# Square, cast and subtraction over two blocks at a time, the second layer in runs of a pair, and row-tiled matmuls behind the last block

## The chip, the cores and the metric

The kernel runs on one core of a Trainium2 chip. TensorE multiplies; VectorE, ScalarE and GpSimd work on tiles in SBUF, the on-chip memory; TensorE writes its results to PSUM, a second on-chip memory of eight banks; SyncE issues the transfers. Each engine takes its instructions in the order in which the program lists them, and waits at an instruction until what it needs is there. The metric is the device time of one execution, in microseconds (us); the profile describes one execution of the program.

## The reference

Four batches of 12480 tokens with 128 channels pass through an attention with 49 agents per batch, and the result goes through a layer with squared relu (d_ff = 2048).

```python
def _attn_ref(q, k, v, agents):
    scale = 1.0 / np.sqrt(q.shape[-1])
    def sm(a, b):
        s = scale * (a @ b.transpose(0, 2, 1))
        s = s - s.max(-1, keepdims=True)
        e = np.exp(s)
        return e / (e.sum(-1, keepdims=True) + 1e-09)
    agent_v = sm(agents, k) @ v
    return sm(q, agents) @ agent_v

def _moe_ref(x, w_in, w_out):
    r = np.maximum(x @ w_in, 0.0)
    return (r * r) @ w_out
```

## The kernel before

**Tiling.** The tokens are cut into 52 stages (NSG) of 960 tokens, 13 per batch, and the 2048 hidden columns into 16 blocks (NF) of 128. The main loop counts blocks: i = 16 * stage + block, 832 in all. A tile of a block holds 128 hidden columns by 960 tokens, as two halves of 480, one PSUM bank each. The values are split in two: a number rounded to the fast matmul type (the high half) and the remainder (the low half), and a product is made of three matmuls: high by high, high by low, low by high.

**One pair of blocks.** `mm1` (line 340) makes the hidden values of blocks i and i+1 in one go: four full matmuls and four that use 32 rows of the array each, side by side. `relu` (354) takes a block out of PSUM on ScalarE, `square` (358) squares it on ScalarE, `high` (362) makes the rounded copy `gh` on VectorE and `low` (366) the remainder `gl` on VectorE. `mm2` (370) multiplies `gh` and `gl` of one block with the second layer's weights `wo_hi` and `wo_lo` and adds into two PSUM banks `out0` and `out1`, six matmuls per block. The first and last block of a stage do the three products of one half and then those of the other; the blocks between do four with `wo_hi` and then two with `wo_lo`. After the last block `store` (392) copies the two banks out, one on ScalarE and one on VectorE, and sends them off. There is one pair of `out` banks, so the next stage's first `mm2` waits for these copies.

**The order.** Nothing is scheduled by a tool: every step is entered with a time by `at` (408), the list is sorted by that time (597), and each engine gets its instructions in this order. Times are in units of blocks, so a period of the loop is two units, from an even i to the next. Lines 583 to 595 enter the steps of the main loop; `mm2` and `store` follow the block by LAG = 4 units.

**The attention.** It is laid between the steps of the main loop. A planner (`chain`, 418; `plan_tokens`, 452; `plan_batch`, 461) gives each step a slot g, a whole number, and enters it at g + .5; no engine has two such steps in a slot. For each stage, `plan_tokens` enters in the slots of the stage before: scores on TensorE (`q_scores`) and `q_max` on VectorE in slot 16n, `q_sub` on VectorE in 16n+1, `q_exp` on ScalarE and `q_sum` on VectorE in 16n+2, `q_inverse` on VectorE in 16n+4, then GpSimd and ScalarE steps, `q_transpose` on TensorE and two `q_copy` on ScalarE in 16n+10 and 16n+11. `plan_batch` spreads the next batch's work over a whole batch: `k_scores`, `k_copy`, `k_pmax` first, then `v_hi` and `v_lo` (ScalarE, VectorE), `v_acc` (TensorE), `v_sum` (VectorE), at the end `a_final` and the folded weights `w_make`. In the last batch only token work is left.

**Buffers.** The pool `ew` holds the tiles of the main loop by tag: `r` (2 buffers), `g` (3), `gh` and `gl` (4 each), of 960 columns. At the start the same buffers serve the weights, which arrive as 64-bit numbers: `raw_load` (71) fetches a piece, `to_f32` (80) turns it into 32 bit on VectorE with work tiles `cv_p` and `cv_x`.

Of the kernel before, what the change touches and what calls it, by code (L numbers as in the profile page):

```python
# [9 lines left out]
F32 = mybir.dt.float32  # L10
BF16 = mybir.dt.bfloat16
F32R = mybir.dt.float32r
U32 = mybir.dt.uint32
AF = mybir.ActivationFunctionType
ALU = mybir.AluOpType
AX = mybir.AxisListType

P = 128
CH = 120
G = 8  # L20
TT = CH * G // 2
# [4 lines left out]
def agent_attention_relu2_kernel(ctx: ExitStack, tc: tile.TileContext, qT, kT, v, agT, w_in, w_out, outT):  # L26
# [6 lines left out]
    nc = tc.nc  # L33
    C, B, NCH, _ = kT.shape
    A = agT.shape[2]
    F = w_in.shape[1]
    NF = F // P
    NS = NCH // G
    A2 = 2 * A
    scale = 1.0 / math.sqrt(C)  # L40

    cpool = ctx.enter_context(tc.tile_pool(name="cpool", bufs=1))
    io = ctx.enter_context(tc.tile_pool(name="io", bufs=6))
    wk = ctx.enter_context(tc.tile_pool(name="wk", bufs=2))
    ew = ctx.enter_context(tc.tile_pool(name="ew", bufs=4))
    ps_h = ctx.enter_context(tc.tile_pool(name="ps_h", bufs=2, space=bass.MemoryType.PSUM))
    ps_o = ctx.enter_context(tc.tile_pool(name="ps_o", bufs=1, space=bass.MemoryType.PSUM))
    ps_a = ctx.enter_context(tc.tile_pool(name="ps_a", bufs=2, space=bass.MemoryType.PSUM))
# [13 lines left out]
    win_sb = cpool.tile([P, F], F32, name="win_sb")  # L62
    wo_hi = cpool.tile([P, NF, P], F32R, name="wo_hi")
    wo_lo = cpool.tile([P, NF, P], F32R, name="wo_lo")
    PW = 512
# [3 lines left out]
    raws = {}  # L69

    def raw_load(t, src):
        raw = ew.tile([P, PW, 2], U32, name="raw", tag="gl")
        raws[t, src is wi_bits] = raw
        if src is wi_bits:
            nc.sync.dma_start(out=raw, in_=wi_bits[:, t * PW:(t + 1) * PW, :])
        else:
            nj = PW // P
            nc.sync.dma_start(out=raw.rearrange("p (j c) w -> p j c w", c=P), in_=wo_bits[:, t * nj:(t + 1) * nj])

    def to_f32(raw, dst):  # L80

        lo, hi = raw[:, :, 0], raw[:, :, 1]
        p = ew.tile([P, PW], U32, name="cv_p", tag="g", bufs=3)
        x = ew.tile([P, PW], F32, name="cv_x", tag="gh")
        ts, stt = nc.vector.tensor_scalar, nc.vector.scalar_tensor_tensor
        return [
            lambda: ts(out=p, in0=hi, scalar1=20, scalar2=0x7FF, op0=ALU.logical_shift_right, op1=ALU.bitwise_and),
            lambda: ts(out=p, in0=p, scalar1=896.0, scalar2=1151.0, op0=ALU.max, op1=ALU.min),  # L90
            lambda: ts(out=p, in0=p, scalar1=896.0, scalar2=float(1 << 23), op0=ALU.subtract, op1=ALU.mult),
            lambda: stt(out=p, in0=hi, scalar=0x80000000, in1=p, op0=ALU.bitwise_and, op1=ALU.bitwise_or),
            lambda: ts(out=x.bitcast(U32), in0=hi, scalar1=0xFFFFF, scalar2=0x100000, op0=ALU.bitwise_and, op1=ALU.bitwise_or),
            lambda: stt(out=x, in0=lo, scalar=2.0 ** -32, in1=x.bitcast(U32), op0=ALU.mult, op1=ALU.add),
            lambda: stt(out=dst, in0=x, scalar=2.0 ** -20, in1=p.bitcast(F32), op0=ALU.mult, op1=ALU.mult),
        ]

    cv, wo = {}, {}

    def win_make(t, step):  # L100
        if step == 0:
            cv["i"] = to_f32(raws.pop((t, True)), win_sb[:, t * PW:(t + 1) * PW])
        cv["i"][step]()

    def wo_make(t, step):
        if step == 0:
            wo[t] = ew.tile([P, PW], F32, name="wo_f", tag="gh")
            cv["o"] = to_f32(raws.pop((t, False)), wo[t])
        cv["o"][step]()

    def wo_split(t, step):
# [20 lines left out]
    kts, vts, pes, pss = {}, {}, {}, {}  # L132
# [4 lines left out]
    def bank():  # L137
        turn[0] += 1
        if many[0] and turn[0] % 2:
            return ps_h.tile([P, 2, 512], F32, name="h")[:, 0]  # L140
        return ps_a.tile([P, 512], F32, name="ps_att")
# [106 lines left out]
    X = 28  # L248
    R = A - X
    K = A2 + X  # L250
    assert K <= P and R <= 32
    W = {}
    w_lo = cpool.tile([A, F], F32R, name="w_lo")

    def w_make(b, f, step):
        sl = slice(f * 512, (f + 1) * 512)
        if f == 0 and step == 0:
            W[b] = (wk.tile([P, F], F32R, name="w_a"), wk.tile([P, NF // 2, P], F32R, name="w_b"))
        wa, wb = W[b]
        if step == 0:  # L260
            pss["w", f] = bank()
            nc.tensor.matmul(pss["w", f][:A2, :], a2, win_sb[:, sl], start=True, stop=True)  # L262
        elif step == 1:
            nc.scalar.copy(wa[:A2, sl], pss["w", f][:A2, :])
        elif step == 2:
            nc.vector.tensor_tensor(w_lo[:, sl], pss.pop(("w", f))[:A, :], wa[:A, sl].bitcast(F32), op=ALU.subtract)
        else:
            nc.sync.dma_start(out=wa[A2:K, sl].bitcast(F32), in_=w_lo[:X, sl].bitcast(F32))
            for r in range(4):
                src = w_lo[X:, sl].rearrange("a (j u p) -> a j u p", u=2, p=P)[:, :, r // 2]  # L270
                eng = nc.scalar if b == 0 and f == 0 and r > 1 else nc.sync
                eng.dma_start(out=wb[32 * r:32 * r + R, 2 * f:2 * f + 2].bitcast(F32), in_=src.bitcast(F32))


    PT, qs, es, mxs, sms, pps = {}, {}, {}, {}, {}, {}
# [57 lines left out]

    NSG = B * NS
    NG = NSG * NF
    hs, rs_, gs, ghs, gls = {}, {}, {}, {}, {}

    outs = {}

# [11 lines left out]
            nc.tensor.matmul(hs[i + r // 2][:, r % 2, :TT], wb[rows, i % NF // 2, :], pb[rows], start=False, stop=True)  # L351

    def relu(i):
        rs_[i] = ew.tile([P, 2, TT], F32, name="r", bufs=2)
        nc.scalar.activation(rs_[i], hs.pop(i)[:, :, :TT], AF.Relu)  # L355

    def square(i):
        gs[i] = ew.tile([P, 2, TT], F32, name="g", bufs=3)
        nc.scalar.activation(gs[i], rs_.pop(i), AF.Square)  # L359

    def high(i):
        ghs[i] = ew.tile([P, 2, TT], F32R, name="gh")
        nc.vector.tensor_copy(ghs[i], gs[i])  # L363

    def low(i):
        gls[i] = ew.tile([P, 2, TT], F32R, name="gl")
        nc.vector.tensor_tensor(out=gls[i], in0=gs.pop(i), in1=ghs[i].bitcast(F32), op=ALU.subtract)  # L367

    def mm2(i):
        s, j = divmod(i, NF)  # L370
        gh, gl = ghs.pop(i), gls.pop(i)
        if j == 0:
            outs[s] = [ps_o.tile([P, 512], F32, name=f"out{t}") for t in range(2)]
        o = outs[s]
        first, last = j == 0, j == NF - 1

        def one(w, x, t, st=False, sp=False):
            nc.tensor.matmul(o[t][:, :TT], w[:, j, :], x[:, t, :], start=st, stop=sp)  # L378

        if first or last:  # L380
            for t in range(2):
                one(wo_hi, gh, t, st=first)
                one(wo_lo, gh, t)
                one(wo_hi, gl, t, sp=last)
        else:
            for t in range(2):
                one(wo_hi, gh, t)
                one(wo_hi, gl, t)
            for t in range(2):
                one(wo_lo, gh, t)  # L390

    def store(s):
        o = outs.pop(s)
# [10 lines left out]
    LAG = 4  # L404
# [3 lines left out]
    def at(t, f, *args):  # L408
        steps.append((t, len(steps), f, args))
# [8 lines left out]
    def chain(t, todo):  # L418
# [29 lines left out]
        return first, t  # L448

    reads_bank = (k_copy, k_pmax, k_max, v_sum, a_final, w_make, q_max, q_sub, q_copy)  # L450

    def plan_tokens(s, base, loaded=False):
# [55 lines left out]
    for n, x, src in ((0, .025, wi_bits), (1, .055, wi_bits), (2, .085, wi_bits), (3, .125, wi_bits),  # L508
                      (0, .325, wo_bits), (1, .355, wo_bits), (2, .385, wo_bits), (3, .415, wo_bits)):
        at(Z + x, raw_load, n, src)  # L510
    for n in range(NS):
        t = Z + 6 + KP * n
# [4 lines left out]
    for x in range(7):  # L517
        for n in range(3):
            at(Z + (9 if (n, x) != (2, 6) else 18) + 6 * n + .8 * x, win_make, n, x)
# [14 lines left out]
    for n in range(NS):  # L534
        t = t0 + 1.84 * n
# [3 lines left out]
    for x in range(7):  # L539
        at(t0 + 2 + .7 * x, win_make, 3, x)  # L540
        for n in range(3):
            at(t0 + 7 + 5 * n + .7 * x, wo_make, n, x)
# [24 lines left out]
    for x in range(7):  # L567
        at(t + 5.5 + .1 * x, wo_make, 3, x)
# [6 lines left out]
    for f in range(2, F // 512):  # L575
        _, e = chain(4 * f - 7, [("PE", w_make, 0, f, 0), ("ACT", w_make, 0, f, 1), ("DVE", w_make, 0, f, 2)])
# [3 lines left out]
    for b in range(1, B):  # L580
        plan_batch(b, (b - 1) * NS * NF, NS * NF)

    for i in range(NG + LAG):
        if i < NG:
            if i % 2 == 0:
                at(i, mm1, i)
                at(i + .1, relu, i)
                at(i + .12, relu, i + 1)
            at(i + .55, square, i)
            at(i + .6, high, i)  # L590
            at(i + (.65 if i % 2 else 1.25), low, i)
        if 0 <= i - LAG < NG:
            at(i + .2, mm2, i - LAG)
            if (i - LAG) % NF == NF - 1:
                at(i + .2, store, (i - LAG) // NF)
    with tc.manual_schedule():
        for _, _, f, args in sorted(steps, key=lambda x: x[:2]):
            f(*args)
# [24 lines left out]
```

## Time and profile before

| | |
|---|---|
| median of 3 runs | 2048.43 us (2046.95 to 2049.32) |
| span of the profiled execution | 2044.0 us |
| granted TensorE clock, mean over the span | 0.997 |
| data moved | 125.16 MB, 61 GB/s on the mean |

The span runs from the first to the last instruction of the profiled execution. "Busy" is the time in which an engine works on an instruction; matmuls overlap one another in the record, so TensorE's busy time alone does not say how near its peak it is. A row of the list of groups gives the source line, engine and operation, what it writes and reads, its shape and its count, then busy time and the mean duration of one instruction in ns, then the engine's idle time ahead of it and who ended it. A row of the timeline gives start, duration, engine, line and operation; "x4" stands for four instructions in a row, and a bracket for idle time ahead of it and what ended that. A row of the busy time by stretch gives the stretch, its length, the busy time (and count) of TensorE, its weight loads, VectorE, ScalarE and GpSimd, then the granted TensorE clock, the share of the DMA engines and GB/s.

### The profile page before, as it was taken

How to read it: one execution, taken by the hardware profiler on the slowest of the kernel's cores; microseconds unless marked ns; L12 is line 12 of the kernel's file. 1: busy time of each engine (PE TensorE's matmuls, PEld its weight loads, DVE VectorE, ACT ScalarE, POOL GpSimd, SP SyncE). 2: the span in 40 equal slices, each digit the busy share in tenths (PEclk: the TensorE clock that was granted, in tenths of full speed). 3: DMA queues.
4: the chain of work that ended last, by engine and by line, in shares of the span. 5: the costliest groups of instructions: out<-in, count | busy, mean ns of one | idle time of the engine just before them, and what ended most of it. 6: DMA issues, size and time to landing. Idle time of an engine off the chain costs nothing.

```text
span 2044.0 us, 30401 instructions
## 1 busy us (share of the span) xinstructions
PE 2024.0 (99%) x11011; PEld 1581.1 (77%) x11017; DVE 1823.7 (89%) x2274; ACT 1729.4 (85%) x2166; POOL 230.2 (11%) x196
## 2 busy tenths in 40 slices
PE   9899999999999999999999999999999999999999
PEld 8678777777777777777778787777777777777777
DVE  7688899999888889999998888999998988989897
ACT  2587889998887888999888888999888888888897
POOL 0100002221000001222100000122210000000000
PEclk9899999999999999999999999999999999999999
DMA  9321212211121212211112211212101111111010
GB/s 312 91 79 54 74 51 63 84 51 35 56 70 53 83 46 68 74 57 58 35 50 76 76 52 60 72 57 70 56 26 50 45 31 45 30 34 39 28 35 25
DMA packets 51446, 125.16 MB, mean 61 GB/s; under 512 B 7072, under 2 KB 16560, under 8 KB 51296
## 3 DMA queue, kind: packets, MB, share of 16 engines
q1 hardware_dynamic: 51198, 123.19, 19.5%
q8 instruction: 86, 1.41, 0.3%
q14 instruction: 64, 0.52, 0.1%
q10 hardware_dynamic: 98, 0.04, 0.0%
HBM read 81.37 MB, written 25.56 MB: 52 GB/s over the span
## 4 chain that ended last, share of the span: by engine, by line
PE 86%; DVE 8%; issue 4%; DMA 1%; ACT 1%; SPq 0%; DVEq 0%; ACTq 0%
PE out L378 51%; PE h L348 16%; PE h L351 8%; PE ps_att L154 3%; PE ps_att L285 3%; DVE gh L363 3%; DVE gl L367 2%; PE ps_att L322 1%; PE ps_att L209 1%; DVE vs L202 1%; DMA vt<-v 1%; PE ps_att L262 1%; PE h L154 0%; ACT g L359 0%; DVE ob L396 0%
## 5 line engine op out<-in xcount | busy, mean ns | idle before, releaser
L367 DVE TENSOR_TENSOR gl<-g,gh 128x960 fp32r<-128x960 f32 x832 | 1016.5, 1222 | 30.6
L355 ACT ACTIVATE r<-h 128x960 f32<-128x960 f32 x832 | 763.8, 974 | 175.9 <-PE h L351 172.2
L359 ACT ACTIVATE g<-r 128x960 f32<-128x960 f32 x832 | 825.3, 1016 | 5.2 <-DVE gl L367 5.2
L378 PE MATMUL out<-gh,wo_hi 128*128 128x480 f32 x1664 | 689.9, 415 | 5.1 <-DVE ob L396 3.6
L363 DVE CAST gh<-g 128x960 fp32r<-128x960 f32 x832 | 583.3, 701 | 97.1 <-ACT g L359 84.5
L378 PE MATMUL out<-gl,wo_hi 128*128 128x480 f32 x1664 | 633.7, 381 | 1.4 <-DVE gl L367 1.0
L378 PE MATMUL out<-gh,wo_lo 128*128 128x480 f32 x1664 | 516.1, 381 | 0.0
L348 PE MATMUL h<-p_a,w_a 126*128 126x480 f32 x1664 | 435.2, 383 | 1.8 <-ACT r L355 1.8
L378 PEld LDWEIGHTS out<-gh,wo_hi 128*128 128x128 f32 x1664 | 313.2, 188 | 141.3 <-issue 71.0
L378 PEld LDWEIGHTS out<-gh,wo_lo 128*128 128x128 f32 x1664 | 312.9, 188 | 49.3
L348 PEld LDWEIGHTS h<-p_a,w_a 126*128 126x128 f32 x1664 | 309.1, 189 | 52.8 <-ACT r L355 2.7
L378 PEld LDWEIGHTS out<-gl,wo_hi 128*128 128x128 f32 x1664 | 313.8, 189 | 41.6 <-DVE gl L367 5.7
L351 PE MATMUL h<-p_b,w_b 21*128 21x480 f32 x1664 | 204.9, 479 | 0.7 <-DMA w_b<-w_lo 0.7
L308 POOL TENSOR_TENSOR e<-e,sm 120x392 f32<-120x392 f32 x52 | 55.0, 1059 | 1322.0 <-DVE sm L305 1197.3
L351 PEld LDWEIGHTS h<-p_b,w_b 21*128 21x128 f32 x1664 | 80.1, 181 | 139.6 <-issue 137.9
L285 PEld LDWEIGHTS ps_att<-ag_sb,qt 128*120 128x120 f32 x832 | 95.2, 185 | 3.7 <-issue 0.2
L285 PE MATMUL ps_att<-ag_sb,qt 128*120 128x49 f32 x832 | 92.7, 264 | 0.0
L154 PEld LDWEIGHTS ps_att<-ag_sb,kt 128*120 128x120 f32 x704 | 80.6, 185 | 3.2 <-PE ps_att L262 0.3
L190 POOL TENSOR_TENSOR pe<-sk,pe 120x392 fp32r<-120x392 f32 x39 | 52.7, 1351 | 235.2 <-ACT pe L187 193.3
L154 PE MATMUL ps_att<-ag_sb,kt 128*120 128x49 f32 x704 | 78.4, 264 | 0.1
L158 ACT COPY sk<-ps_att 120x392 f32<-120x392 f32 x44 | 21.4, 487 | 63.7 <-PE ps_att L154 63.7
L315 POOL TENSOR_TENSOR pp<-e,pp 120x392 fp32r<-120x392 f32 x52 | 55.6, 1070 | 163.2 <-ACT pp L312 158.9
(93 smaller groups left out, 939.5 us busy)
## 6 DMA issues: line engine op xcount, KB each, us to landing
vt<-v SPq DMA_DIRECT2D x104, 243.8 KB
kt<-kT SPq DMA_DIRECT2D x52, 480.0 KB
qt<-qT SPq DMA_DIRECT2D x52, 480.0 KB
outT<-ob SPq DMA_DIRECT2D x51, 480.0 KB
p_b<-p_a SPq DMA_DIRECT2D x208, 39.4 KB
p_a<-p_a SPq DMA_DIRECT2D x52, 105.0 KB
raw<-w_in SPq DMA_DIRECT2D x4, 512.0 KB
raw<-w_out SPq DMA_DIRECT2D x4, 512.0 KB
```

Source lines behind the costliest of these rows:

```text
L154: nc.tensor.matmul(ps[:CH, c * A:(c + 1) * A], kt[:, c, :], ag_sb[:, b, :], start=True, stop=True)
L190: eng.tensor_tensor(out=pes[n][:, :, A:], in0=piece(n), in1=pes[n][:, :, :A].bitcast(F32), op=ALU.subtract)
L285: nc.tensor.matmul(ps[:CH, c * A:(c + 1) * A], qt[:, c * CH:(c + 1) * CH], ag_sb[:, s // NS, :], start=True, stop=True)
L308: eng.tensor_tensor(out=es[s], in0=es[s], in1=sms.pop(s).to_broadcast([CH, G, A]), op=ALU.mult)
L315: eng.tensor_tensor(out=pps[s][:, :, A:], in0=es.pop(s), in1=pps[s][:, :, :A].bitcast(F32), op=ALU.subtract)
L348: nc.tensor.matmul(hs[x][:, t, :TT], wa[:K, (x % NF) * P:(x % NF + 1) * P], pa[:K, t, :], start=True, stop=False)
L351: nc.tensor.matmul(hs[i + r // 2][:, r % 2, :TT], wb[rows, i % NF // 2, :], pb[rows], start=False, stop=True)
L355: nc.scalar.activation(rs_[i], hs.pop(i)[:, :, :TT], AF.Relu)
L359: nc.scalar.activation(gs[i], rs_.pop(i), AF.Square)
L363: nc.vector.tensor_copy(ghs[i], gs[i])
L367: nc.vector.tensor_tensor(out=gls[i], in0=gs.pop(i), in1=ghs[i].bitcast(F32), op=ALU.subtract)
L378: nc.tensor.matmul(o[t][:, :TT], w[:, j, :], x[:, t, :], start=st, stop=sp)
```

## The change

- `relu` writes two blocks into one tile `g` of two blocks; `square`, `high` and `low` run once per pair, on 1920 columns. `square` works in place.
- `mm2` runs once per pair, twelve matmuls in one run: first the four that use `gh` of each block, then those that use `gl`. In the first and last pair of a stage, all six products of one half of the tokens come first and then those of the other half; between them, each product is done for both halves in turn.
- In the list of steps, `square` stands at i+1.7, `high` at i+2.6 and `low` at i+3.1 (before: .55, .6 and .65 or 1.25 after the block); `mm2` of the pair stays at i+4.2 and `store` stands at 1.3 instead of .2.
- The tags `gh` and `gl` move to a pool `eh` with two buffers of a pair; `g` has three. The raw weights, the work tiles of `to_f32` and `w_lo` are laid into the new buffers.
- A new function `row_tiles` issues 28 small matmuls on parts of the rows, behind everything else. Nothing reads what they write.

```diff
     def raw_load(t, src):
-        raw = ew.tile([P, PW, 2], U32, name="raw", tag="gl")
+        raw = ew.tile([P, PW, 2], U32, name="raw", tag="g") if len(raws) % 5 < 3 else eh.tile([P, PW, 2], U32, name="raw", tag="gl")
...
     def relu(i):
-        rs_[i] = ew.tile([P, 2, TT], F32, name="r", bufs=2)
-        nc.scalar.activation(rs_[i], hs.pop(i)[:, :, :TT], AF.Relu)
+        if i % 2 == 0:
+            gs[i] = ew.tile([P, 2, 2, TT], F32, name="g")
+        nc.scalar.activation(gs[i - i % 2][:, i % 2], hs.pop(i)[:, :, :TT], AF.Relu)
 
     def square(i):
-        gs[i] = ew.tile([P, 2, TT], F32, name="g", bufs=3)
-        nc.scalar.activation(gs[i], rs_.pop(i), AF.Square)
+        nc.scalar.activation(gs[i], gs[i], AF.Square)
 
     def high(i):
-        ghs[i] = ew.tile([P, 2, TT], F32R, name="gh")
+        ghs[i] = eh.tile([P, 2, 2, TT], F32R, name="gh")
         nc.vector.tensor_copy(ghs[i], gs[i])
 
     def low(i):
-        gls[i] = ew.tile([P, 2, TT], F32R, name="gl")
+        gls[i] = eh.tile([P, 2, 2, TT], F32R, name="gl")
         nc.vector.tensor_tensor(out=gls[i], in0=gs.pop(i), in1=ghs[i].bitcast(F32), op=ALU.subtract)
...
-        first, last = j == 0, j == NF - 1
...
+        first, last = j == 0, j == NF - 2
+        todo = [(w, gh, u) for u in range(2) for w in (wo_hi, wo_lo)] + [(wo_hi, gl, u) for u in range(2)]
         if first or last:
-            for t in range(2):
-                one(wo_hi, gh, t, st=first)
-                one(wo_lo, gh, t)
-                one(wo_hi, gl, t, sp=last)
-        else:
-            for t in range(2):
-                one(wo_hi, gh, t)
-                one(wo_hi, gl, t)
-            for t in range(2):
-                one(wo_lo, gh, t)
+            order = [(n, t) for t in range(2) for n in range(6)]
+        else:
+            order = [(n, t) for n in range(6) for t in range(2)]
+        for n, t in order:
+            w, x, u = todo[n]
+            nc.tensor.matmul(o[t][:, :TT], w[:, j + u, :], x[:, u, t, :], start=first and n == 0, stop=last and n == 5)
+
+    def row_tiles():
...
+        last = PT[NSG - 1][0][:, 0, :]
+        for j in range(6):
+            one(0, 0, 64, j)
+            one(1, 64, 62, j)
...
-    for i in range(NG + LAG):
+    for i in range(0, NG + LAG, 2):
         if i < NG:
-            if i % 2 == 0:
-                at(i, mm1, i)
-                at(i + .1, relu, i)
-                at(i + .12, relu, i + 1)
-            at(i + .55, square, i)
-            at(i + .6, high, i)
-            at(i + (.65 if i % 2 else 1.25), low, i)
-        if 0 <= i - LAG < NG:
+            at(i, mm1, i)
+            at(i + .1, relu, i)
+            at(i + .12, relu, i + 1)
+            at(i + 1.7, square, i)
+            at(i + 2.6, high, i)
+            at(i + 3.1, low, i)
+        if i >= LAG:
             at(i + .2, mm2, i - LAG)
-            if (i - LAG) % NF == NF - 1:
-                at(i + .2, store, (i - LAG) // NF)
+            if (i - LAG) % NF == NF - 2:
+                at(i + 1.3, store, (i - LAG) // NF)
+    at(NG + LAG, row_tiles)
```

More of the change, by code (lines that the diff above doesn't have):

```diff
@@ L44, in agent_attention_relu2_kernel @@
     wk = ctx.enter_context(tc.tile_pool(name="wk", bufs=2))
-    ew = ctx.enter_context(tc.tile_pool(name="ew", bufs=4))
+    ew = ctx.enter_context(tc.tile_pool(name="ew", bufs=3))
+    eh = ctx.enter_context(tc.tile_pool(name="eh", bufs=2))
     ps_h = ctx.enter_context(tc.tile_pool(name="ps_h", bufs=2, space=bass.MemoryType.PSUM))
@@ L78, in raw_load, with to_f32 @@
             nc.sync.dma_start(out=raw.rearrange("p (j c) w -> p j c w", c=P), in_=wo_bits[:, t * nj:(t + 1) * nj])
-    def to_f32(raw, dst):
+    def to_f32(raw, work, dst):
         lo, hi = raw[:, :, 0], raw[:, :, 1]
-        p = ew.tile([P, PW], U32, name="cv_p", tag="g", bufs=3)
-        x = ew.tile([P, PW], F32, name="cv_x", tag="gh")
+        p, x = work[:, 0].bitcast(U32), work[:, 1]
         ts, stt = nc.vector.tensor_scalar, nc.vector.scalar_tensor_tensor
@@ L101, in win_make @@
         if step == 0:
-            cv["i"] = to_f32(raws.pop((t, True)), win_sb[:, t * PW:(t + 1) * PW])
+            cv["i"] = to_f32(raws.pop((t, True)), eh.tile([P, 3, PW], F32, name="cv", tag="gh"), win_sb[:, t * PW:(t + 1) * PW])
         cv["i"][step]()
@@ L106, in wo_make @@
         if step == 0:
-            wo[t] = ew.tile([P, PW], F32, name="wo_f", tag="gh")
-            cv["o"] = to_f32(raws.pop((t, False)), wo[t])
+            work = eh.tile([P, 3, PW], F32, name="cv", tag="gh")
+            wo[t] = work[:, 2]
+            cv["o"] = to_f32(raws.pop((t, False)), work, wo[t])
         cv["o"][step]()
@@ L252, in agent_attention_relu2_kernel @@
     W = {}
-    w_lo = cpool.tile([A, F], F32R, name="w_lo")
+    w_lo = {}
     def w_make(b, f, step):
@@ L265, in w_make @@
         elif step == 2:
-            nc.vector.tensor_tensor(w_lo[:, sl], pss.pop(("w", f))[:A, :], wa[:A, sl].bitcast(F32), op=ALU.subtract)
+            w_lo[f] = wk.tile([A, 512], F32R, name="w_lo")
+            nc.vector.tensor_tensor(w_lo[f], pss.pop(("w", f))[:A, :], wa[:A, sl].bitcast(F32), op=ALU.subtract)
         else:
-            nc.sync.dma_start(out=wa[A2:K, sl].bitcast(F32), in_=w_lo[:X, sl].bitcast(F32))
+            nc.sync.dma_start(out=wa[A2:K, sl].bitcast(F32), in_=w_lo[f][:X].bitcast(F32))
             for r in range(4):
-                src = w_lo[X:, sl].rearrange("a (j u p) -> a j u p", u=2, p=P)[:, :, r // 2]
+                src = w_lo[f][X:].rearrange("a (j u p) -> a j u p", u=2, p=P)[:, :, r // 2]
                 eng = nc.scalar if b == 0 and f == 0 and r > 1 else nc.sync
@@ L335, in agent_attention_relu2_kernel @@
     NG = NSG * NF
-    hs, rs_, gs, ghs, gls = {}, {}, {}, {}, {}
+    hs, gs, ghs, gls = {}, {}, {}, {}
     outs = {}
@@ L374, in mm2, with one @@
         o = outs[s]
-        first, last = j == 0, j == NF - 1
-        def one(w, x, t, st=False, sp=False):
-            nc.tensor.matmul(o[t][:, :TT], w[:, j, :], x[:, t, :], start=st, stop=sp)
+        first, last = j == 0, j == NF - 2
+        todo = [(w, gh, u) for u in range(2) for w in (wo_hi, wo_lo)] + [(wo_hi, gl, u) for u in range(2)]
         if first or last:
-            for t in range(2):
-                one(wo_hi, gh, t, st=first)
-                one(wo_lo, gh, t)
-                one(wo_hi, gl, t, sp=last)
-        else:
-            for t in range(2):
-                one(wo_hi, gh, t)
-                one(wo_hi, gl, t)
-            for t in range(2):
-                one(wo_lo, gh, t)
+            order = [(n, t) for t in range(2) for n in range(6)]
+        else:
+            order = [(n, t) for n in range(6) for t in range(2)]
[3 more added lines that the diff above has]
+    def row_tiles():
+        a, b = [ps_h.tile([P, 2, 512], F32, name="h") for _ in range(2)]
+        banks4 = [a[:, 0, :TT], a[:, 1, :TT], b[:, 0, :TT], b[:, 1, :TT]]
+        def one(bank, lo, n, j):
+            nc.tensor.matmul(banks4[bank], wo_hi[lo:lo + n, j, :], last[lo:lo + n], start=True, stop=True)
+        last = PT[NSG - 1][0][:, 0, :]
+        for j in range(6):
+            one(0, 0, 64, j)
+            one(1, 64, 62, j)
+        for r in range(4):
+            one(r, 32 * r, 32 if r < 3 else 30, r)
+        for j in range(2):
+            one(0, 0, 64, j)
+            one(2, 64, 32, j)
+            one(3, 96, 30, j)
+        for j in range(2):
+            one(0, 0, 64, j)
+            one(1, 64, 62, j)
+        for j in range(2):
+            one(2, 0, K, j)
     def store(s):
```

## The prediction

> **What bounds the kernel now.** I read the shares of busy time on the page first, then the busy time of each engine by stretch.
>
> ```profile
> span 2044.0 us, 30401 instructions
> ...
> PE 2024.0 (99%) x11011; PEld 1581.1 (77%) x11017; DVE 1823.7 (89%) x2274; ACT 1729.4 (85%) x2166; POOL 230.2 (11%) x196
> ```
>
> ```profile
> 1100.00:1600.00 500.00, 497.85 (x2698) 388.68 (x2698) 454.98 (x559) 436.16 (x551) 66.28 (x53) 1.00 0.19 56
> 1600.00:2000.00 400.00, 400.00 (x2090) 309.92 (x2089) 358.30 (x432) 353.16 (x421) 22.71 (x22) 1.00 0.11 35
> ```
>
> TensorE (first busy figure of a row) is the bound everywhere: idle for 2.15 us of 500 in a stage with batch work, not at all where only token work is left. VectorE (third) is about 90% busy and ScalarE (fourth) 87 to 88%, but they wait for TensorE, not the reverse. So saved VectorE and ScalarE time is worth nothing by itself. What counts is whether TensorE still finds its operands ready. Next, one undisturbed pair of blocks in the timeline, TensorE and then ScalarE.
>
> ```profile
> 1786.39 1.03 PE L348 MATMUL h<-p_a,w_a 126*128 126x480 f32 x4
> ...
> 1787.77 0.49 PE L378 MATMUL out<-gh,wo_hi 128*128 128x480 f32 x1
> 1788.10 0.38 PE L378 MATMUL out<-gl,wo_hi 128*128 128x480 f32 x1
> 1788.32 0.38 PE L378 MATMUL out<-gh,wo_hi 128*128 128x480 f32 x1
> ...
> 1790.51 1.04 PE L348 MATMUL h<-p_a,w_a 126*128 126x480 f32 x4
> ```
>
> ```profile
> 1787.93 1.84 ACT L355 ACTIVATE r<-h 128x960 f32<-128x960 f32 x2 [0.47 <-PE h L351]
> 1789.65 1.91 ACT L359 ACTIVATE g<-r 128x960 f32<-128x960 f32 x2
> ```
>
> Call the start of mm1 of the pair T. The next T is 4.12 later (1790.51 - 1786.39). mm2 begins at T+1.38; its second matmul comes 0.33 on, each later one 0.22 on. The relus begin at T+1.54, the squares at T+3.26.
>
> **Part by part.** The matmuls of a pair stay the same in number and shape; their new order costs nothing that I can price, since equal and unequal neighbours both stand 0.22 apart above. Fused square, cast and subtraction save instructions on engines that TensorE does not wait for: zero, as long as the gate below is met. What matters is the **new place** of `high` and `low` in VectorE's order. Before, both run in the pair's own period (times i+.55 to i+1.65) and mm2 reads them at i+4.2. After, `high(i)` stands at i+2.6 and `low(i)` at i+3.1, mm2 still at i+4.2. So in period i, VectorE's order is: item of the even slot (i+.5), high(i-2), low(i-2), item of the odd slot; and in the very next period mm2(i-2) reads them. At the same time TensorE's slot items of period i now run after all twelve mm2 matmuls (i+.2), at the end of the period. An even-slot item that waits for TensorE or ScalarE now holds up the halves that TensorE needs 1.4 us later. Before, the same wait had a period of slack.
>
> First the durations for 1920 columns. The cast and the subtraction of 960 columns take 0.65 and 1.16 us in the rows below; a cast of 128 columns and a subtraction of 512 (0.69) give the slopes.
>
> ```profile
> 387.39 0.69 DVE L202 TENSOR_TENSOR vs<-vt,vs 120x512 fp32r<-120x512 f32 x1
> 387.99 0.65 DVE L363 CAST gh<-g 128x960 fp32r<-128x960 f32 x1
> ```
>
> ```profile
> L198 ACT CAST vs<-vt 120x512 fp32r<-120x512 f32 x78 | 49.8, 638 | 0.0
> ...
> L158 ACT COPY sk<-ps_att 120x392 f32<-120x392 f32 x44 | 21.4, 487 | 63.7 <-PE ps_att L154 63.7
> ...
> L55 DVE CAST ident_r<-ident 128x128 fp32r<-128x128 f32 x1 | 0.2, 228 | 0.0
> ```
>
> Cast: 0.65 + 960 x (0.65-0.23)/832 = 1.14. Subtraction: 1.16 + 960 x (1.16-0.69)/448 = 2.17. Twice the old instruction, 1.30 and 2.32, is the upper bound. Both are estimates from these rows. Undisturbed, the squares now end at T+3.26+1.85 = T+5.11, high at T+6.3 and low at T+8.5, with mm2's first matmul at 8.24+1.38 = 9.62 and its first `gl` four (first and last pair of a stage) or eight (other pairs) matmuls later. That fits, with nothing lost.
>
> Now with a token's scores. The rows are TensorE, VectorE and ScalarE around one `q_scores`:
>
> ```profile
> 1722.82 1.78 PE L285 MATMUL ps_att<-ag_sb,qt 128*120 128x49 f32 x16
> 1724.43 0.47 PE L378 MATMUL out<-gh,wo_hi 128*128 128x480 f32 x1
> 1724.73 0.38 PE L378 MATMUL out<-gl,wo_hi 128*128 128x480 f32 x1
> ```
>
> ```profile
> 1724.64 0.57 DVE L290 TENSOR_REDUCE mx<-ps_att 120x8 f32<-120x392 f32 x1 [0.82 <-PE ps_att L285]
> 1725.12 0.65 DVE L363 CAST gh<-g 128x960 fp32r<-128x960 f32 x1
> 1725.81 1.16 DVE L367 TENSOR_TENSOR gl<-g,gh 128x960 fp32r<-128x960 f32 x1
> 1726.89 0.56 DVE L294 TENSOR_TENSOR e<-ps_att,mx 120x392 f32<-120x392 f32 x1
> ...
> 1729.65 0.56 DVE L301 TENSOR_REDUCE sm<-e 120x8 f32<-120x392 f32 x1 [0.44 <-ACT e L297]
> 1730.54 0.66 DVE L363 CAST gh<-g 128x960 fp32r<-128x960 f32 x1 [0.33 <-ACT g L359]
> 1731.12 0.65 DVE L396 COPY ob<-out 128x480 f32<-128x480 f32 x1
> ```
>
> ```profile
> 1729.08 0.53 ACT L297 ACTIVATE e<-e 120x392 f32<-120x392 f32 x1
> ```
>
> `q_max` already waits for TensorE (0.82). It starts 0.21 after the matmul behind the scores; the cast follows 0.48 after its start; a dependent start comes 0.04 after the end before it; and a VectorE instruction that depends on nothing starts 0.08 before the end of the one ahead (1725.81 + 1.16 against 1726.89). How fast TensorE resumes after VectorE shows in an old wait of this kind: the copy ends at 399.21, the matmul starts at 399.26, 0.05 later.
>
> ```profile
> 398.56 0.65 DVE L396 COPY ob<-out 128x480 f32<-128x480 f32 x1
> ```
>
> ```profile
> 399.26 0.48 PE L378 MATMUL out<-gh,wo_hi 128*128 128x480 f32 x1 [0.55 <-DVE ob L396]
> ```
>
> *q_max.* Count from the mm1 matmul behind the scores, which is the next T. q_max 0.21; high 0.69 to 1.83; low 1.87 to 4.04; `gl` usable at 4.09. TensorE wants it at 1.38 + 0.33 + 3x0.22 = 2.37, plus 0.08 since a matmul behind scores takes 0.30, not 0.22: 2.45. The token's slot is 16n, so mm2(i-2) is the last pair of its stage, where `gl` is fifth. Loss 1.64 each. Walking the planner's rules (lines 452 to 483) gives 50 such slots: 24 with nothing of TensorE in the odd slot, 6 with a short step (about 0.3 less), 15 with `v_acc` (0.96 less, rows below), 5 with `k_scores` (1.61 less). Sum 24x1.64 + 6x1.34 + 15x0.68 = 57.6 us.
>
> ```profile
> 400.01 1.12 PE L209 MATMUL ps_att<-vs,pe 120*98 120x258 f32 x8
> 400.97 0.38 PE L378 MATMUL out<-gh,wo_hi 128*128 128x480 f32 x1
> ```
>
> *q_sum.* Same origin. q_sub follows low at 3.96 and ends at 4.52; q_exp 4.56 to 5.09; q_sum 5.13; high 5.61 to 6.75; low 6.79 to 8.96, usable at 9.01. The next T is 4.12 + 0.08 + 1.64 = 5.84; mm2 there is the first pair of a stage and wants `gl` at 5.84 + 2.37 = 8.21: loss 0.80. Its second half also waits for the store's copy, which VectorE now makes after low: 8.88 + 0.65 + 0.05 = 9.58 against 9.01 + 0.44: 0.13 more. 47 slots (three others have scores behind them) x 0.93 = 43.7 us.
>
> *v_lo.* v_hi takes the place of the square, T+3.26 to 3.90; v_lo 3.94; high 4.54 (0.60 on, as at 387.39) to 5.68; low 5.72 to 7.89, usable 7.94. Wanted at 4.12 + 1.38 + 0.33 + 7x0.22 = 7.37: loss 0.57. 27 even slots have it with its v_hi and without TensorE work; nine pairs are neighbours and pay once: 18 x 0.57 = 10.3 us. *k_pmax* behind scores and k_copy: k_copy 0.21 to 0.70, k_pmax 0.74, high 1.22, low 2.40 to 4.57, usable 4.62, wanted 3.33: 11 x 1.29 = 14.2 us. *w_make* is alike in three slots, about 4 us.
>
> New waits: 57.6 + 43.7 + 10.3 + 14.2 + 4 = 130 us. Old waits of TensorE go: three batch stages idle 2.15 us each, and late weight loads stretch some more; I take 10 (between 6.5 and 20). The tail: the last low ends about 0.9 later than its half did, and 28 row-tiled matmuls follow the last mm2.
>
> ```profile
> 2039.94 0.37 PE L378 MATMUL out<-gl,wo_hi 128*128 128x480 f32 x1
> ```
>
> At 0.22 each they end 6.2 after 2040.2, 2.4 beyond the span's end; side by side in fourteen steps they end inside it. With the 0.9, I take 2. The start (other raw buffers, same load order, never fewer free) I put at 0, within 3 either way. Sum: 2044.0 + 130 - 10 + 2 = 2166. The median shown, 2048.4, stands 4.4 above the profiled span, so **2170**.
>
> **Rivals.** *The clock falls.* The granted clock has halved after short idleness here:
>
> ```profile
> 80.52:83.93 3.41, 1.62 (x6) 0.40 (x3) 2.58 (x4) 3.41 (x5) 1.20 (x1) 1.00 0.00 0
> 83.93:90.76 6.83, 6.82 (x19) 4.92 (x20) 6.69 (x11) 5.37 (x7) 0.16 (x1) 0.50 0.02 4
> ```
>
> A stretch with 1.62 of 3.41 us busy was followed by 6.83 us at 0.50. A q_max loss of 1.64 leaves about 1.77 of 3.41 busy. If all 24 full ones tripped it, each would add half of 3.41 to 6.83, so 1.7 to 3.4: 41 to 82 us, 2211 to 2252. The wait comes in two pieces, which seldom fall in one such stretch. The Trainium skill ("TensorE: Matmul & The Clock Gate", Part 1) has the clock halve only after a whole idle window of about 3.4 us; by that rule nothing trips and 2170 stands. The row above differs, so the rival keeps its chance.
>
> *Less is lost.* Each late low also delays the next T, which gives later waits slack; if half of the waits vanish so: 2105. *More:* the fused instructions take twice the old ones: 0.31 on some 125 waits, 39 us, 2209.
>
> *Faster.* The item ahead of `high` does not hold it, because the waits are reached late anyway or the order of issue is not the order of the listing. Then VectorE per pair does 3.3 instead of 3.53 (2 x (0.69+1.08)), the old waits go, and the time is 2044 - 10 + 2 + 4.4 = 2040. It decides if `gl` is usable within 2.45 us of the scores' end; my sum has 4.09. The Trainium skill ("VectorE: DVE Perf Modes", The TRN2 errata) has a fixed cost per instruction that larger tiles pay once, which by itself points to this outcome; the slopes above agree with a fixed part (0.16 us in a subtraction), but TensorE is the bound. *The change does nothing:* the slack of one period suffices: 2047.
>
> **How the numbers follow.** Chances: forecast 0.68 (2140 to 2212, which covers *more*), clock 0.09, less lost 0.13, faster 0.07, nothing 0.03. The likeliest gives 2170. Leaving out faster, nothing, the lower part of *less* and the upper part of *clock*: 2110 to 2235. A measurement of this kernel tells about 0.2% from no change. Faster 0.07, same 0.03, slower 0.90.
>
> **What would show it.** Right: waits of TensorE for `gl` and `gh` in the list of waits, some 130 us in about 125 pieces, up to 1.7 each, at T+1.4 and T+2.4 behind every q_scores; TensorE busy well below 97%; VectorE waiting several us for TensorE before `mx`; quiet pairs still at 4.1. Wrong: `gh` casts ahead of `mx` in VectorE's order, quiet pairs longer than 4.2 (the new matmul order costs), or the granted clock below 1.00 in the main loop.

## The result

| | time, us | ratio to the kernel before |
|---|---|---|
| before | 2048.46 median (2046.95 to 2049.32, 4 runs) | 1 |
| changed | 2220.93 median (2219.37 to 2223.33, 4 runs) | 1.0841, 95% interval 1.0825 to 1.0856 |

The change makes the kernel 172 us slower. The forecast was slower, 2170 us, with a range of 2110 to 2235: direction and range hold, the size is 51 us short. First the page and groups of the changed kernel; after a group's busy time and mean come its idle time and what ended it.

```profile
span 2221.6 us, 27723 instructions
...
PE 2091.1 (94%) x11039; PEld 1584.6 (71%) x11045; DVE 1713.7 (77%) x1442; ACT 1711.6 (77%) x1750; POOL 337.4 (15%) x196
...
L366 DVE TENSOR_TENSOR gl<-g,gh 128x1920 fp32r<-128x1920 f32 x416 | 941.2, 2263 | 28.9 <-DVE gh L362 0.5
...
L289 DVE TENSOR_REDUCE mx<-ps_att 120x8 f32<-120x392 f32 x52 | 29.5, 567 | 179.1 <-PE ps_att L284 179.1
```

VectorE works 110 us less than before (1713.7 against 1823.7) and yet the span is 178 us longer. TensorE, the bound, fell from 99% to 94%. Idle time ahead of `mx` rose from 30.1 us, in the row of before below, to 179.1 us:

```profile
L290 DVE TENSOR_REDUCE mx<-ps_att 120x8 f32<-120x392 f32 x52 | 29.3, 564 | 30.1 <-PE ps_att L285 30.1
```

VectorE now stands at `q_max` for 3.5 us on the mean, with the cast and subtraction that TensorE needs queued behind it. The list of waits (who waited for whom, us in total, times, longest) shows the other half of that circle:

```profile
DVE mx L289 <- PE ps_att L284: 179.1, 51, 5.2
...
PE out L382 <- DVE gl L366: 78.7, 140, 1.1
...
PE out L382 <- DVE gh L362: 40.1, 67, 1.4
```

Before, TensorE had one such row in the main loop, for `gl`, and none for `gh`:

```profile
PE out L378 <- DVE gl L367: 1.0, 3, 0.4
```

(In the record a matmul of 0.38 us runs on for 0.16 us after the next one, 0.22 later, has started, so these waits look shorter than they are; the gaps between the starts of matmuls give more, below.) One token in the timeline, TensorE and then VectorE:

```profile
1876.19 1.78 PE L284 MATMUL ps_att<-ag_sb,qt 128*120 128x49 f32 x16
1877.80 1.11 PE L347 MATMUL h<-p_a,w_a 126*128 126x480 f32 x4
1878.84 0.49 PE L350 MATMUL h<-p_b,w_b 21*128 21x480 f32 x4
1879.70 0.48 PE L382 MATMUL out<-gh,wo_hi 128*128 128x480 f32 x1 [0.37 <-DVE gh L362]
1880.02 0.38 PE L382 MATMUL out<-gh,wo_lo 128*128 128x480 f32 x1
1880.24 0.38 PE L382 MATMUL out<-gh,wo_hi 128*128 128x480 f32 x1
1880.45 0.38 PE L382 MATMUL out<-gh,wo_lo 128*128 128x480 f32 x1
1881.89 0.70 PE L382 MATMUL out<-gl,wo_hi 128*128 128x480 f32 x2 [1.06 <-DVE gl L366]
1882.43 0.38 PE L382 MATMUL out<-gh,wo_hi 128*128 128x480 f32 x1
```

```profile
1878.02 0.57 DVE L289 TENSOR_REDUCE mx<-ps_att 120x8 f32<-120x392 f32 x1 [4.60 <-PE ps_att L284]
1878.50 1.15 DVE L362 CAST gh<-g 128x1920 fp32r<-128x1920 f32 x1
1879.68 2.16 DVE L366 TENSOR_TENSOR gl<-g,gh 128x1920 fp32r<-128x1920 f32 x1
1881.76 0.56 DVE L293 TENSOR_TENSOR e<-ps_att,mx 120x392 f32<-120x392 f32 x1
1882.91 0.56 DVE L300 TENSOR_REDUCE sm<-e 120x8 f32<-120x392 f32 x1 [0.60 <-ACT e L296]
```

The matmul with `gl` starts 4.09 after the mm1 behind the scores (1881.89 - 1877.80), the figure of the prediction; `q_max` waited 4.60 us. A quiet pair takes 4.11 us (1896.98 - 1892.87), against 4.12 before, so the new order of the matmuls costs nothing there:

```profile
1892.87 1.04 PE L347 MATMUL h<-p_a,w_a 126*128 126x480 f32 x4
...
1896.98 1.04 PE L347 MATMUL h<-p_a,w_a 126*128 126x480 f32 x4
```

For the terms of the sum I took every gap between the starts of two matmuls of mm2, and from mm1 to mm2, less its usual length (0.22, 0.33 or 0.41 us), and put it down to VectorE's even-slot item of the period before:

| item | predicted, us | measured, us |
|---|---|---|
| q_max | 57.6 | 72.1 |
| q_sum and the store's copy | 43.7 | 46.8 |
| v_lo | 10.3 | 36.2 |
| k_pmax | 14.2 | 16.8 |
| w_make | 4 | 9.6 |
| sum | 130 | 181.5 |

The prediction counted 18 paying slots of `v_lo` and three of `w_make`; by the same gaps 42 and seven paid.

### The profile page after: what moved, and what is told of

Same layout as the page of the kernel before. It is cut to its first block, busy times and chain, and to the rows that moved or that the text cites. A ratio compares the mean times of both kernels' runs of the same rounds, so it can differ in the third digit from the quotient of the medians.

```text
span 2221.6 us, 27723 instructions
## 1 busy us (share of the span) xinstructions
PE 2091.1 (94%) x11039; PEld 1584.6 (71%) x11045; DVE 1713.7 (77%) x1442; ACT 1711.6 (77%) x1750; POOL 337.4 (15%) x196
## 4 chain that ended last, share of the span: by engine, by line
PE 60%; DVE 28%; ACT 7%; issue 4%; DMA 1%; SPq 0%; DVEq 0%; ACTq 0%
PE out L382 35%; DVE gl L366 14%; PE h L347 9%; DVE gh L362 8%; PE h L350 4%; PE ps_att L284 4%; PE ps_att L152 3%; ACT g L355 3%; DVE vs L200 2%; ACT g L358 2%; PE ps_att L321 1%; DVE mx L289 1%; DVE sm L300 1%; ACT e L296 1%; DVE e L293 1%
## 5 line engine op out<-in xcount | busy, mean ns | idle before, releaser
L366 DVE TENSOR_TENSOR gl<-g,gh 128x1920 fp32r<-128x1920 f32 x416 | 941.2, 2263 | 28.9 <-DVE gh L362 0.5
L355 ACT ACTIVATE g<-h 128x960 f32<-128x960 f32 x832 | 762.5, 972 | 210.3 <-PE h L350 208.2
L358 ACT ACTIVATE g<-g 128x1920 f32<-128x1920 f32 x416 | 755.1, 1815 | 4.4
L382 PE MATMUL out<-gh,wo_hi 128*128 128x480 f32 x1664 | 584.8, 412 | 41.2 <-DVE gh L362 40.1
L362 DVE CAST gh<-g 128x1920 fp32r<-128x1920 f32 x416 | 495.2, 1190 | 104.7 <-ACT g L358 100.6
L382 PE MATMUL out<-gl,wo_hi 128*128 128x480 f32 x1664 | 470.5, 395 | 79.3 <-DVE gl L366 78.7
L289 DVE TENSOR_REDUCE mx<-ps_att 120x8 f32<-120x392 f32 x52 | 29.5, 567 | 179.1 <-PE ps_att L284 179.1
L314 POOL TENSOR_TENSOR pp<-e,pp 120x392 fp32r<-120x392 f32 x52 | 112.1, 2156 | 202.1 <-ACT pp L311 196.5
L324 ACT CAST p_a<-ps_att 98x480 fp32r<-98x480 f32 x103 | 52.7, 563 | 85.1 <-PE ps_att L321 85.1
L200 DVE TENSOR_TENSOR vs<-vt,vs 120x512 fp32r<-120x512 f32 x78 | 77.7, 1011 | 42.3 <-ACT vs L196 42.3
```

The lines of the kernel that those rows point to most:

```text
L200: eng.tensor_tensor(out=vs[:, :, C + 2:], in0=vts[n][:, halves[h], :C], in1=vs[:, :, :C].bitcast(F32), op=ALU.subtract)
L314: eng.tensor_tensor(out=pps[s][:, :, A:], in0=es.pop(s), in1=pps[s][:, :, :A].bitcast(F32), op=ALU.subtract)
L355: nc.scalar.activation(gs[i - i % 2][:, i % 2], hs.pop(i)[:, :, :TT], AF.Relu)
L358: nc.scalar.activation(gs[i], gs[i], AF.Square)
L382: nc.tensor.matmul(o[t][:, :TT], w[:, j + u, :], x[:, u, t, :], start=first and n == 0, stop=last and n == 5)
```

## The experiments

The theory: VectorE's order is the cause, that is, an item that waits stands ahead of the cast and subtraction whose result TensorE needs next. Rivals: instructions of 1920 columns are too coarse for the lag, wherever they stand; the clock; the new order of the matmuls. All times below are medians; the changed kernel has 2220.93.

**The halves ahead of the item.**

```diff
-            at(i + 2.6, high, i)
-            at(i + 3.1, low, i)
+            at(i + 2.4, high, i)
+            at(i + 2.45, low, i)
```

> The changed kernel with the cast and the subtraction of a pair put ahead of VectorE's even-slot item instead of behind it (times 2.4 and 2.45 instead of 2.6 and 3.1); nothing else. Theory (the order on VectorE is the cause): the waits of TensorE for gh and gl, some 180 us in the changed kernel, go nearly all; 2035 to 2060 us, and TensorE busy 98% or more. Rival (instructions of 1920 columns are too coarse for a lag of two periods, wherever they stand): at least half of the loss stays, over 2130 us. Rival (the clock or the new order of the matmuls costs): little changes, over 2180 us.

Measured 2047.28 us (2044.66 to 2050.75), ratio to the kernel before 0.9995, interval 0.9985 to 1.0004. Two numbers in the list of steps give back the whole loss, with 1920-column instructions, mm2 in runs of a pair and the tail left in. That rules out the coarse instructions and the matmul order as causes by themselves; whether instructions of 960 columns would lose less in the changed kernel's place was not tried. Its waits and, as busy time by stretch, its main loop:

```profile
PE out L382 <- DVE gh L362: 4.8, 6, 1.2
...
PE out L382 <- DVE gl L366: 2.4, 7, 0.9
```

```profile
100.00:2000.00 1900.00, 1893.57 (x10194) 1479.84 (x10195) 1612.98 (x1301) 1626.35 (x1665) 272.12 (x178) 1.00 0.18 54
```

TensorE is busy for 1893.57 of 1900 us, VectorE for 85%. The saving on VectorE buys nothing.

**Only q_max and q_sum behind the subtraction.**

```diff
-                at(g + .5, f, *args)
+                at(g + (1.2 if f in (q_max, q_sum) and g % 2 == 0 else .5), f, *args)
```

> The changed kernel with q_max and q_sum alone put behind the subtraction of their period (time 1.2 instead of .5 of an even slot). Theory: the two token terms of the sum go, in the trace of the changed kernel about 72 and 47 us, the rest stays: 2221 less 105 to 120, so 2100 to 2116 us. Rival (coarse instructions): no part of the loss belongs to these two items; over 2190 us.

Measured 2097.43 us (2097.23 to 2097.80): 123.5 less, 3.5 us more than the most that was expected. The two terms are real. Of the 4.6 us beyond their gaps (118.9), some 3 lie at `v_lo`, whose term is 33 us here. The record of this run has no stretch at half clock (3.41 us at a granted clock of 0.50) after the start of the main loop, where that of the changed kernel has ten; those ten all lie at `q_max` or `q_sum`, so their cost is in the two terms already.

**Only v_lo behind the subtraction.** As above, with `f is v_lo`.

> The changed kernel with the even-slot v_lo alone put behind the subtraction. Theory: the v_lo term goes. The prediction put it at 10 us, the gaps between matmuls in the trace of the changed kernel give 36: 2185 to 2190 us by the trace, 2211 by the prediction. Rival: no change, 2221 us.

Measured 2201.71 us (2198.05 to 2202.75): 19 less, between the two forecasts. The term in the gaps fell from 36.2 to 10.1. Part came back: waits at `q_max` with `v_acc` behind it rose from 12.3 to 16.9 us.

**TensorE's item ahead of mm2.**

```diff
-                at(g + .5, f, *args)
+                at(g + (.15 if e == "PE" and g % 2 == 0 else .5), f, *args)
```

> The changed kernel with TensorE's even-slot items ahead of the twelve mm2 matmuls of the period instead of behind them (time .15 instead of .5); VectorE's order stays as changed. Theory: what VectorE's items wait for is there 2.7 us earlier, so the q_max, k_pmax and even w_make terms go (72, 17 and some 8 us in the trace), q_sum rises from 0.9 to about 1.4 each (20 us more), v_lo stays: 2221 less 75, so 2130 to 2160 us. Rival (only VectorE's order matters, not when TensorE's items run): 2221 us.

Measured 2123.41 us (2122.62 to 2125.48): 97.5 less, a third more than the 75 expected and below the range given, and the wait at `q_sum` rose to 1.47 on the mean, as expected. So both halves of the change's order count: VectorE's item ahead of the halves, and TensorE's item at the end of the period. One stretch at half clock is left in the loop.

**The last pair of a stage in the middle order**, so `gl` comes ninth and not fifth.

```diff
-        if first or last:
+        if first:
```

> The changed kernel with the last pair of a stage in the order of the middle pairs, so that its first product with gl is the ninth matmul, not the fifth. The prediction's sum taken term by term: q_max loses 0.87 less on 30 stages and 0.8 on 15, 38 us, so 2183 us. Theory (the next term follows on VectorE's chain low, q_sub, q_exp, q_sum, high, low, which does not move, while TensorE arrives earlier): the q_sum wait grows by as much, and 2210 to 2222 us is measured; of the stretches at half clock some may go.

Measured 2223.00 us (2214.57 to 2223.63): no gain, as the theory had it, though 1 us above its range. TensorE of this run, one token:

```profile
1880.87 1.14 PE L382 MATMUL out<-gl,wo_hi 128*128 128x480 f32 x4 [0.18 <-DVE gl L366]
1881.85 1.04 PE L347 MATMUL h<-p_a,w_a 126*128 126x480 f32 x4
1882.82 0.49 PE L350 MATMUL h<-p_b,w_b 21*128 21x480 f32 x4
1883.66 0.45 PE L382 MATMUL out<-gh,wo_hi 128*128 128x480 f32 x1 [0.35 <-DVE gh L362]
...
1885.77 0.70 PE L382 MATMUL out<-gl,wo_hi 128*128 128x480 f32 x2 [0.99 <-DVE gl L366]
```

The bracket ahead of the first `gl` shrinks from 1.06 to 0.18, and one period later 0.35 and 0.99 stand where the changed kernel has:

```profile
1885.12 0.49 PE L382 MATMUL out<-gh,wo_hi 128*128 128x480 f32 x1
...
1886.79 0.70 PE L382 MATMUL out<-gl,wo_hi 128*128 128x480 f32 x2 [0.53 <-DVE gl L366]
```

Over the whole run the gaps say the same: the q_max term falls from 72 to 26 us and the q_sum term rises from 46 to 96. The time is set by VectorE's chain (q_max, high, low, q_sub, then ScalarE's q_exp, q_sum, high, low). A wait taken away in front of it only moves to its end.

**Zeros in the wait.**

```diff
+            if last and n == 4 and t == 0:
+                for _ in range(3):
+                    nc.tensor.matmul(o[0][:, :TT], zz[:, :P], zz[:, :TT], start=False, stop=False)
```

> The changed kernel with three extra matmuls of zeros (added to out0, so they change no value) between the products with gh and those with gl of the last pair of every stage, where TensorE waits for gl behind q_scores: some 0.65 us of work in a wait of 0.8 to 1.2 us; 5 of 50 stages have no such wait and get 3 us longer together. Theory that the idle time trips the clock: the trace of the changed kernel has nine stretches of 3.41 us at half clock in the main loop; most go, 9 x 1.7 less 3, so about 2207 to 2212 us. Rival (the stretches come of something else): they stay, 2221 to 2226 us.

Measured 2215.73 us (2213.53 to 2217.37): 5.2 less although work was added, which lies between the two forecasts. Nine of the ten stretches at half clock are gone, so it was the idle time that brought them on. The zeros cost next to nothing: in the five stages without a wait the gaps of the pair grow by 0.55 us each, and the q_sum wait behind it shrinks by as much. So the nine stretches were worth some 5 us, about 0.6 each; I had put 1.7. The gaps of the changed kernel show why it is so little. A half-clock stretch adds 0.9 to 1.2 us to a pair, but where it falls on a q_max pair, as seven did, TensorE needs VectorE's next result that much later: behind six of the seven the q_sum wait, else 0.90 us, is gone.

**Without k_sub.** The body of `k_sub` returns at once when GpSimd is to run it.

> The changed kernel without GpSimd's k_sub (the scores of the agents are not shifted by their maximum in batches 1 to 3); all slots stay as planned. Theory (the v_lo term came out at 36 us instead of 10 since VectorE's v_lo and subtraction run longer beside GpSimd work): the v_lo waits that follow a long GpSimd step shrink, 8 to 20 us less: 2200 to 2213 us, and v_lo takes nearer 0.7 than 1.0 us on the mean. Rival (neighbouring slots alone make the term): 2219 to 2223 us with v_lo still at 1.0 us.

Measured 2211.07 us (2209.62 to 2213.82): 9.9 less, v_lo's term 36.2 down to 27.2, and its duration back to what it was before the change. First the row of the kernel before, then of the changed kernel, then of this run:

```profile
L202 DVE TENSOR_TENSOR vs<-vt,vs 120x512 fp32r<-120x512 f32 x78 | 62.5, 802 | 0.0
```

```profile
L200 DVE TENSOR_TENSOR vs<-vt,vs 120x512 fp32r<-120x512 f32 x78 | 77.7, 1011 | 42.3 <-ACT vs L196 42.3
```

```profile
L202 DVE TENSOR_TENSOR vs<-vt,vs 120x512 fp32r<-120x512 f32 x78 | 61.7, 805 | 46.2 <-ACT vs L198 46.2
```

**Without the row-tiled matmuls, halves ahead.** The edit of the first experiment and `row_tiles` left out.

> The changed kernel with the cast and subtraction ahead of the even-slot item (as in halves_first) and without the 28 row-tiled matmuls behind the last block. Theory: in the trace of the changed kernel these matmuls end 0.9 us before the span does, in step with the last store, so they cost 0 to 2 us: 2045 to 2047 us, ratio to the kernel before 0.998 to 1.000. Rival (a tail cost of 5 us): 2042 us.

Measured 2048.11 us (2045.20 to 2050.00, 11 runs), ratio 0.9993, interval 0.9984 to 1.0002. The tail costs nothing that can be told, and no version here beats the kernel before.

## Why the prediction was right, and where it was short

The mechanism was right, but 2221 lies above 2212, the end of the interval that the prediction gives to the forecast itself. The whole range reached to 2235 because it took in the lower part of the clock rival; what filled that room was mostly `v_lo`, not the clock. That the range holds is in part luck.

- **TensorE is the bound; time saved elsewhere is worth nothing.** Right: with the halves ahead VectorE has 1714.0 us busy against 1823.7, and the time is that of before.
- **The new place of `high` and `low`.** Right, and shown from both sides: moving the halves or the two token items ends the loss or its larger part; moving TensorE's items ends more than half.
- **Durations for 1920 columns.** 1.14 and 2.17 us were predicted; 1.15 and 2.16 stand in the token above. The bound of twice the old instruction was not needed.
- **q_max and q_sum.** The place and the arrival of `gl` (4.09) are right to a hundredth. The q_max term came out 14.5 us larger, mostly by two costs. After a wait the second matmul comes 0.33 and not 0.22 later, which I left out: in the token above the two behind the wait take 0.54 (1882.43 - 1881.89). Over the 151 waits for `gl` that is 16 us of the 181.5, 5 of them at q_max; a full q_max loss is 1.76 and not 1.64. And the half clock adds 7 us to seven q_max pairs. The q_sum term is nearly right in part by luck: of the 47 waits put at 0.93 each, 36 take 0.90, the five behind `k_scores` take 2.06 or more, and the six behind a q_max pair at half clock are nothing. That q_max and q_sum form one chain was in the sum; `last_turns` shows it.
- **v_lo, the mis-sized term: 36 us for 10.** The step that failed is the count of 18 payments ("nine pairs are neighbours and pay once"), with undisturbed durations. All 42 even slots with v_lo paid: the 18 counted ones 17.5 us and not 10.3, the nine neighbours 11.4, and the 15 that the sum left out (nine without a `v_hi` in the slot, six with `v_acc` in the next) 7.1. So TensorE paid twice at neighbours, and VectorE was slower beside GpSimd. In the timeline of the changed kernel, VectorE and then GpSimd:

```profile
1027.67 2.73 DVE L366 TENSOR_TENSOR gl<-g,gh 128x1920 fp32r<-128x1920 f32 x1
1030.33 2.81 DVE L200 TENSOR_TENSOR vs<-vt,vs 120x512 fp32r<-120x512 f32 x2
1033.07 1.15 DVE L362 CAST gh<-g 128x1920 fp32r<-128x1920 f32 x1
```

```profile
1028.34 4.25 POOL L178 TENSOR_TENSOR sk<-sk,mM 120x392 f32<-120x392 f32 x2
```

  Beside `k_sub` the subtraction takes 2.73 (2.16 alone) and two v_lo 2.81 (0.69 each alone), so the cast ends at 1034.22 and TensorE stands for 1.38 us. The mean of v_lo in the trace of before, 802 ns against 0.69 in the row quoted in the prediction, held the warning. `no_ksub` puts about 10 us on this one step of GpSimd; what the other GpSimd steps cost was not tried. With the halves ahead v_lo takes 1087 ns on the mean, more still, and the time is that of before: a slow v_lo costs only where the halves stand behind it.
- **The clock.** The rival had 0.09, with all 24 full q_max waits at half clock, and a clock below 1.00 in the main loop was to be a sign of being wrong. Ten stretches came in the loop, worth some 5 us by `zero_fill`. They lie on a grid of 3.41 us. In the busy time by stretch (second figure TensorE, the figure ahead of the last two the granted clock) stand one stretch, the one behind it, and the same for a wait that the clock did not answer:

```profile
634.84:638.25 3.41, 1.79 (x11) 0.90 (x9) 3.38 (x4) 3.38 (x4) 0.00 (x0) 1.00 0.02 5
638.25:641.66 3.41, 3.41 (x9) 2.85 (x10) 3.34 (x5) 1.77 (x1) 1.58 (x1) 0.50 0.63 189
...
1030.78:1034.19 3.41, 2.11 (x12) 1.32 (x10) 3.41 (x3) 2.90 (x3) 1.82 (x2) 1.00 0.00 0
1034.19:1037.61 3.42, 3.08 (x14) 2.36 (x15) 3.25 (x3) 0.57 (x1) 0.00 (x0) 1.00 0.00 0
```

  With 1.79 busy the next stretch is at 0.50; with 2.11 it is not. Over all stretches of the grid in this run from 100 us on, the three up to 1.81 were followed by half clock, those from 1.98 to 2.03 in seven of twelve cases, those from 2.05 in none. The border is not a sharp one: in `last_turns` two stretches with 2.10 and 2.13 were followed by half clock (at 974.99 and 425.37 us), and in `vlo_after` one with 1.71 was not (at 639.17). By the rule of the Trainium skill ("TensorE: Matmul & The Clock Gate", Part 1), which asks for a whole idle window, none of the ten would have come; the measurement decides.
- **Old waits, start and tail** (-10, 0, +2). With the halves ahead, with the tail or without it, the median is that of before within 0.1%. The terms of 181.5 against a span that grew by 177.6 (2221.6 - 2044.0) leave about -4 for the three together, where -8 was put; the single parts lie below what these runs can tell.

The sum: 130 predicted, 181.5 measured; the 51 us between them are nearly all of the gap between 2170 and 2221. Restarts (16) and half clock (5) are in the terms; most of the rest is v_lo.

## What to carry to other kernels

When instructions are fused on an engine that is not the bound, the place of the fused one in its engine's order matters more than the time it saves: ask which waiting instruction stands ahead of it, who waits for it, and how much of a period is left between the two. Where a chain of steps on the off-bound engines sets the time, taking away the first wait moves it to the next; put the operands of the bound engine ahead of anything that waits.

## What the runs showed of the hardware

- The clock halved for 3.41 us behind stretches of the grid with some 1.8 to 2.0 us busy of 3.41, also where the idle time came in two pieces. In the changed kernel none with more than 2.03 was followed by it, in `last_turns` two with 2.10 and 2.13 were. Three matmuls of zeros in the wait did away with nine of the ten.
- A matmul stream that has waited for its operand needs about 0.11 us more to come back to its usual spacing (0.33 and then 0.22).
- VectorE's subtraction of two SBUF tiles of 512 columns took 0.69 us alone and 1.4 us each beside GpSimd's `k_sub`. In the changed kernel `k_sub` took 0.95 us in the 15 cases where no such subtraction (`v_lo` or `low`) ran beside it and 2.87 in the middle of the 21 cases where one did all along, so each slows the other.
